# Moving the start addresses of the stationary operands from 224 to 192 bytes modulo 256 in a channel-attention and squared-ReLU kernel

## The chip, the core and the metric

The kernel runs on one core of one Trainium2 chip. The metric is the device time of one execution in microseconds (us). SBUF, the on-chip memory, is addressed per partition in bytes; "modulo 256" below speaks of those addresses. TensorE (PE) multiplies: each product has a **stationary** (fixed) operand, a block of 128 x 128 that is loaded into the array first, and a **moving** operand, whose columns then stream through. VectorE is DVE in the profile, ScalarE is ACT, GpSimd is POOL, and SP issues most DMAs.

## What is computed

Four batches of channel attention, and on its output a feed-forward layer with squared ReLU:

```python
B, N, C = 4, 6080, 256          # q, k, v: (B, N, C); w_in: (256, 2048); w_out: (2048, 256)
qn = q / (norm(q, axis=1) + 1e-06)
kn = k / (norm(k, axis=1) + 1e-06)
a = softmax(kn.transpose(0, 2, 1) @ qn / tau)      # 256 x 256 for each batch
x = (v @ a).reshape(B * N, C)
h = maximum(x @ w_in, 0.0)
out = (h * h) @ w_out
```

## The kernel before, in words

The softmax matrix is multiplied into `w_in` once for each batch, so that a token needs only `v @ W` (W is 256 x 2048), the ReLU, the square and the product with `w_out`. Every large product is made in three passes: an operand is split into a high part, rounded to float32r, and a low part, and hi x hi, lo x hi and hi x lo are summed in PSUM. Float32r products go through the array at one pass each; the few plain float32 products count twice in the trace.

The work has these stages. First come the Gram matrix of batch 0 (`gram`, plain float32, 256 columns), its norms (`ps_n`), the softmax, and W for batch 0 (`ps_w`, lines 749 to 766: the transposed exponentials `eT_hi` and `eT_lo` are stationary, a 512-column piece of `w_in` moves). Next come two blocks of 512 tokens in plain form (`ps_h` and `ps_o`, 512 columns). All further token blocks go through a two-by-two block scheme with seven products in place of eight, for W (`ps_b`, `ps_h`, `ps_c`) and for `w_out` (`ps_o`), with 256 moving columns, or 240 in the last two blocks of each batch. `PERIOD` (from line 1305) lists the steps of one group of this scheme by hand, and each engine keeps the order of the program. Beside it run the Gram matrices and the softmax of batches 1 to 3 (`gram<-qk_parts`, and `ps_w` with `dec_w` and `acc_w` moving).

Where a tile lies in SBUF follows from the pools, which are laid one behind another in the order in which they are opened: `smalls`, `const`, `wpool`, `wsums`, `pool`. A tile takes a multiple of 32 bytes in each partition, so that the one-column tiles `tau_sb` and `exp_bias` (lines 118 and 120) take 32 bytes each, as does `rinv_room` (line 125). With these in front, `wo_hi` begins at byte 17,888 = 69 x 256 + 224, and as the tiles behind it are multiples of 1,024 bytes, so do `wo_lo`, the weights `wf` (in `wpool`), `wS`, `wS_odd` and `wi` (in `wsums`) and the first tile of `pool`, `qk_parts`, at 224 modulo 256.

Lines 127 to 155 hold that first tile of `pool`: two halves of 4,096 bytes with a gap of `GAP = 8` words, 32 bytes, between them. For the Gram matrices the first half holds the k part (stationary, at 224) and the second the q part (moving). Because of the gap the second half, and every tile of `pool` behind it, begins at 0 modulo 256: the moving operands `v_hi`, `v_lo`, `A`, `s`, `dec_w` and `acc_w`, and also `eT_hi` and `eT_lo` (lines 733 and 734). A stationary block of 128 columns is 512 bytes and a moving one of 256 columns 1,024 bytes, so that slices of a tile keep its remainder. Only slices of 240-column tiles (960 bytes) begin at 0, 64, 128 or 192.

So the operands stand like this before (counts of products from the program, plain float32 ones left out):

| products | count | stationary at | moving at |
|---|---|---|---|
| 256 columns (`ps_b`, `ps_h`, `ps_c`, `ps_o`, `gram<-qk_parts`) | 13,578 | 224 | 0 |
| 240 columns (`ps_b`, `ps_h`, `ps_c`, `ps_o`, `ps_end`) | 2,694 | 224 | 0, 64, 128 or 192 |
| 512 columns (`ps_h`, `ps_o`) | 384 | 224 | 0 |
| 512 columns (`ps_w` of batch 0, `wi` moving) | 48 | 0 | 224 |
| 512 columns (`ps_w` of batches 1 to 3) | 144 | 0 | 0 |

The lines that decide this:

```python
tau_sb = const.tile([P, 1], F32, name="tau_sb")                      # 118
exp_bias = const.tile([P, 1], F32, name="exp_bias")                  # 120
GAP = 8                                                              # 128
return pool.tile([P, 2 * HALF + GAP], dt, tag="qk_parts", ...)       # 132
eT_hi = pool.tile([P, NC, C], F32R, tag="eT_hi", ...)                # 733
eT_lo = pool.tile([P, NC, C], F32R, tag="eT_lo", ...)                # 734
```

Of the kernel before, what the change touches and what calls it, by code (L numbers as in the profile page):

```python
# [10 lines left out]
F32 = mybir.dt.float32  # L11
F32R = mybir.dt.float32r
# [20 lines left out]
def kernel(  # L33
# [26 lines left out]
    P = 128  # L60
    B, N, C = q.shape
    F = w_in.shape[1]
    NC = C // P
# [35 lines left out]
    const = ctx.enter_context(tc.tile_pool(name="const", bufs=1))  # L99
    wpool = ctx.enter_context(tc.tile_pool(name="wpool", bufs=NG))  # L100
    wsums = ctx.enter_context(tc.tile_pool(name="wsums", bufs=1))
    pool = ctx.enter_context(tc.tile_pool(name="pool", bufs=2))
# [12 lines left out]
    make_identity(nc, ident)  # L115
    ones = const.tile([P, P], F32, name="ones")
    vector.memset(ones, 1.0)
    tau_sb = const.tile([P, 1], F32, name="tau_sb")

    exp_bias = const.tile([P, 1], F32, name="exp_bias")  # L120
    vector.memset(exp_bias, -896.0 * 2.0**23)

    for _ in range(7):
# [1 line left out]
    rinv_room = const.tile([P, NC], F32, name="rinv_room")  # L125

    HALF = NC * GRP
    GAP = 8

    def parts_room(name, dt):  # L130

        return pool.tile([P, 2 * HALF + GAP], dt, tag="qk_parts", name=name, bufs=1)

# [5 lines left out]
    def two_parts(name, dt, shape):  # L139

        room = parts_room(name, dt)
        halves = room[:, 0:HALF], room[:, HALF + GAP :]
        return [half.rearrange("p (a b) -> p a b", a=shape[1]) if len(shape) > 2 else half for half in halves]

    def rounded_qk(name):
# [3 lines left out]
        for at in (0, J * C):  # L149
            of_k = room[:, at : at + J * C]  # L150
            both = bass.AP(of_k.tensor, of_k.offset, [of_k.ap[0], [HALF + GAP, 2], of_k.ap[1]])
            parts.append(both.rearrange("p a (j c) -> p a j c", j=J))
# [438 lines left out]
    def attention(b):  # L591
# [41 lines left out]
        while behind:  # L633
            yield
        yield from softmax_and_W(b)
        while forming:
            yield
# [3 lines left out]
    def step(b, first, point):  # L641

        if b == 0:
            for i in range(first):
                yield i > 0
        else:
            yield
            yield from until(*ALSO.get(point, (point,)))

    def softmax_and_W(b):  # L650
# [79 lines left out]
                    ps_t[:, d * C + h * P : d * C + (h + 1) * P], e[:, h, d * P : (d + 1) * P], ident  # L730
                )
        yield from step(b, 2, "dve")
        eT_hi = pool.tile([P, NC, C], F32R, tag="eT_hi", name=f"eT_hi{b}", bufs=1)
        eT_lo = pool.tile([P, NC, C], F32R, tag="eT_lo", name=f"eT_lo{b}", bufs=1)
        ps_tv = ps_t.rearrange("p (d c) -> p d c", d=NC)
        vector.tensor_copy(eT_hi, ps_tv)
        vector.tensor_sub(eT_lo, ps_tv, eT_hi.bitcast(F32))
# [3 lines left out]
        for g in range(NG):  # L741
            if b == 0:
                while g not in wi_first:
                    yield
                hi, lo = wi_first.pop(g)
# [3 lines left out]
            else:  # L749
                hi, lo = wi_next.pop((b, g))  # L750
# [599 lines left out]
    weights = Weights()  # L1350
    rest = start_first()
    first = softmax_and_W(0)
    heads, squares_of_heads = head_products(), head_squares()
    stage = lambda item: lambda: weights.stage(item)
# [46 lines left out]
    for i in range(PAIR):  # L1401
        part = i % 2
        b, n, f = steps[i]
# [131 lines left out]
    b, n, _ = groups[END]  # L1535
# [53 lines left out]
```

## Time and profile before

| what | value |
|---|---|
| median of 3 runs | 2096.15 us (2094.93 to 2096.56) |
| span of the profiled execution | 2095.3 us |
| PE busy | 2090.3 us (100%) |
| PE weight loads (PEld) busy | 2054.0 us (98%) |
| DVE busy | 1904.2 us (91%) |
| ACT busy | 1878.4 us (90%) |
| POOL busy | 350.1 us (17%) |
| DMA | 549.78 MB, 262 GB/s on the mean |

The profiled execution's own time is its span, from the first to the last instruction; it lies 0.85 us under the median of the runs. The profile gives each matmul a duration of some 280 ns, but matmuls overlap in the array: what counts is the step from the start of one to the start of the next. The chain of waits shows it, since there a piece of n products of one kind stands with the time until the next kind takes over: time divided by n is the step. An L29 in a row is the line of a helper that records every operation, so that rows are told apart by the names of their tiles.

### The profile page before, as it was taken

The page shows a single profiled execution, that of the slowest core. Times are in us where ns is not written, and L with a number is a line of the kernel's source. Part 1 is how long each engine was busy: PE and PEld are TensorE (multiplying, and loading weights), DVE is VectorE, ACT ScalarE, POOL GpSimd, SP SyncE. Part 2 cuts the span into 40 slices and gives each one's busy share as a digit, 9 for nine tenths or more (in the row PEclk, how much of TensorE's full clock was granted, in tenths as well). Part 3 has the DMA queues.
Part 4 walks back from the last instruction along what each step waited for, and adds up shares of the span by engine and source line. Part 5 has one row for each costly group of instructions (what it writes and reads, how often), then busy time and mean ns, then how long its engine had stood idle before and what let it go on. Part 6 is the DMA issues. An engine that isn't in the chain of part 4 may idle for free.

```text
span 2095.3 us, 43463 instructions
## 1 busy us (share of the span) xinstructions
PE 2090.3 (100%) x17158; PEld 2054.0 (98%) x17158; DVE 1904.2 (91%) x2195; ACT 1878.4 (90%) x2379; POOL 350.1 (17%) x430
## 2 busy tenths in 40 slices
PE   9999999999999999999999999999999999999999
PEld 8789999999999999999999999999999999999999
DVE  7898999989999999989998999998999888888887
ACT  5888999889999999889989999998988988988987
POOL 0000121111122111111112111211121121121112
PEclk9999999999999999999999999999999999999999
DMA  9777887889999888789999988878999788787785
GB/s 359 225 227 272 256 258 250 239 260 308 304 279 306 268 256 256 237 247 293 290 298 275 317 251 265 251 241 250 289 280 301 236 240 255 233 246 246 234 241 155
DMA packets 258012, 549.78 MB, mean 262 GB/s; under 512 B 26672, under 2 KB 113072, under 8 KB 257808
## 3 DMA queue, kind: packets, MB, share of 16 engines
q1 hardware_dynamic: 201456, 469.02, 65.2%
q0 software_dynamic: 56352, 77.98, 18.8%
q8 instruction: 135, 2.21, 0.4%
q14 instruction: 69, 0.57, 0.1%
HBM read 433.59 MB, written 58.72 MB: 235 GB/s over the span
## 4 chain that ended last, share of the span: by engine, by line
PE 100%; DVE 0%; DVEq 0%; issue 0%
PE ps_o L29 45%; PE ps_c L29 18%; PE ps_h L29 14%; PE ps_b L29 12%; PE gram L29 7%; PE ps_w L29 2%; PE ps_end L29 0%; PE ps_first L29 0%; PE ps_n L29 0%; PE ps_t L29 0%; DVE x L29 0%; DVE end_o L29 0%; DVEq L1585 0%; DVE ones L29 0%; DVE exp_bias L29 0%
## 5 line engine op out<-in xcount | busy, mean ns | idle before, releaser
L29 DVE TENSOR_TENSOR x<-x 128x1024 f32<-128x1024 f32 (+2 forms) x549 | 465.3, 848 | 11.1
L29 PE MATMUL ps_c<-v_hi,wf 128*128 128x256 f32 (+1 forms) x2208 | 474.5, 279 | 0.2 <-DVE x L29 0.2
L29 POOL DMA_DIRECT2D o<-o x225 | 232.6, 1188 | 1391.2 <-ACT o L29 889.5
L29 DVE TENSOR_TENSOR s_lo<-x,s_hi 128x1024 fp32r<-128x1024 f32 (+1 forms) x366 | 441.9, 1208 | 15.9 <-ACT s_hi L29 15.4
L29 ACT ACTIVATE x<-x 128x1536 f32<-128x1536 f32 (+4 forms) x384 | 405.5, 1056 | 38.5 <-DVE x L29 35.3
L29 ACT CAST s_hi<-x 128x1024 fp32r<-128x1024 f32 (+1 forms) x366 | 383.0, 1046 | 53.9 <-DVE x L29 52.8
L29 DVE TENSOR_TENSOR A_lo<-x,A_hi 128x1536 fp32r<-128x1536 f32 (+2 forms) x183 | 313.6, 1714 | 82.0 <-ACT A_hi L29 67.4
L29 PEld LDWEIGHTS ps_c<-v_hi,wf 128*128 128x128 f32 x2208 | 375.5, 188 | 1.6 <-DVE x L29 0.9
L29 PE MATMUL ps_b<-v_hi,wf 128*128 128x256 f32 (+1 forms) x1472 | 315.9, 278 | 0.0
L29 PE MATMUL ps_h<-v_hi,wf 128*128 128x256 f32 (+1 forms) x1472 | 315.7, 278 | 0.0
L29 PE MATMUL ps_c<-v_lo,wf 128*128 128x256 f32 (+1 forms) x1104 | 307.3, 278 | 0.0
L29 ACT CAST A_hi<-x 128x1536 fp32r<-128x1536 f32 (+2 forms) x183 | 264.4, 1445 | 0.0
L29 PEld LDWEIGHTS ps_h<-v_hi,wf 128*128 128x128 f32 x1472 | 250.5, 188 | 0.0
L29 PEld LDWEIGHTS ps_b<-v_hi,wf 128*128 128x128 f32 x1472 | 250.3, 188 | 0.1
L29 PEld LDWEIGHTS ps_c<-v_lo,wf 128*128 128x128 f32 x1104 | 207.7, 188 | 0.1
L29 PE MATMUL ps_h<-v_lo,wf 128*128 128x256 f32 (+1 forms) x736 | 204.9, 278 | 0.0
L29 PE MATMUL ps_b<-v_lo,wf 128*128 128x256 f32 (+1 forms) x736 | 204.8, 278 | 0.0
L29 PE MATMUL ps_o<-A_hi,wo_hi 128*128 128x256 f32 (+1 forms) x897 | 192.8, 279 | 0.0
L29 PE MATMUL ps_o<-A_hi,wo_lo 128*128 128x256 f32 (+1 forms) x897 | 192.1, 278 | 0.0
L29 PE MATMUL ps_o<-A_lo,wo_hi 128*128 128x256 f32 (+1 forms) x897 | 191.8, 278 | 0.0
L29 PE MATMUL ps_o<-s_hi,wS_hi 128*128 128x256 f32 (+1 forms) x549 | 153.2, 279 | 0.0
L29 PE MATMUL ps_o<-s_hi,wS_lo 128*128 128x256 f32 (+1 forms) x549 | 153.2, 279 | 0.0
(172 smaller groups left out, 5153.5 us busy)
## 6 DMA issues: line engine op xcount, KB each, us to landing
wf<-wf_kept SPq DMA_DIRECT2D x368, 512.0 KB, 5.3
wf<-wf_kept SPq DMA_DIRECT2D x368, 384.0 KB, 4.9
o<-o POOLq DMA_DIRECT2D x114, 256.0 KB, 5.3
qk<-in_k SPq DMA_DIRECT2D x88, 256.0 KB, 5.3
qk<-in_q SPq DMA_DIRECT2D x88, 256.0 KB, 5.4
v<-in_vT SPq DMA_DIRECT2D x76, 256.0 KB, 4.8
out_T<-o POOLq DMA_DIRECT2D x152, 128.0 KB, 5.0
wf_kept<-wS SPq DMA_DIRECT2D x64, 256.0 KB, 7.2
```

Of the source, the lines that this page charges most:

```text
L29: return lambda *args, **kwargs: self.tc.keep_in_program_order(issue(*args, **kwargs))
```

## The change

It puts the two one-column tiles `tau_sb` and `exp_bias` into one tile of two columns, which takes 32 bytes in place of 64. All that lies behind moves down by 32 bytes: `wo`, `wf`, `wS`, `wS_odd`, `wi` and the k half of `qk_parts` now begin at 192 modulo 256. The gap in `qk_parts` grows from 32 to 64 bytes, so that the q half and the tiles behind it still begin at 0. The transposed exponentials `eT_hi` and `eT_lo` move from `pool` to `wsums`, and so from 0 to 192. In the table above 224 becomes 192, and the 0 of `eT` becomes 192 (with `wi` moving at 192 beside it in batch 0). The instructions of each engine, their order and their sizes stay the same.

```diff
-    tau_sb = const.tile([P, 1], F32, name="tau_sb")
-
-    exp_bias = const.tile([P, 1], F32, name="exp_bias")
+    single = const.tile([P, 2], F32, name="single")
+    tau_sb, exp_bias = single[:, 0:1], single[:, 1:2]
     vector.memset(exp_bias, -896.0 * 2.0**23)
...
     HALF = NC * GRP
-    GAP = 8
+    GAP = 16
...
-        eT_hi = pool.tile([P, NC, C], F32R, tag="eT_hi", name=f"eT_hi{b}", bufs=1)
-        eT_lo = pool.tile([P, NC, C], F32R, tag="eT_lo", name=f"eT_lo{b}", bufs=1)
+        eT_hi, eT_lo = (wsums.tile([P, NC, C], F32R, tag=f"eT_{i}", name=f"eT_{i}{b}", bufs=1) for i in ("hi", "lo"))
```

## Rows read from the trace of the kernel before

**Rows 1.** The page's part 1: busy time and share of the span.
```profile
span 2095.3 us, 43463 instructions
PE 2090.3 (100%) x17158; PEld 2054.0 (98%) x17158; DVE 1904.2 (91%) x2195; ACT 1878.4 (90%) x2379; POOL 350.1 (17%) x430
```

**Rows 2.** The page's part 4: the chain that ended last, by engine.
```profile
PE 100%; DVE 0%; DVEq 0%; issue 0%
```

**Rows 3.** The waits of PE: who waited for whom, us, times, longest.
```profile
PE ps_first L29 <- DVE exp_bias L29: 1.1, 1, 1.1
PE ps_c L29 <- DVE x L29: 0.2, 1, 0.2
```

**Rows 4.** Busy time by stretch, one row: busy us (count), clock, DMA share, GB/s.
```profile
1000.00:2080.00 1080.00, 1080.00 (x9256) 1076.55 (x9254) 978.31 (x1082) 980.27 (x1244) 202.95 (x247) 1.00 0.85 260
```

**Rows 5.** The chain, 917 to 933 us: start, us, what (256 columns; ps_w 512).
```profile
920.37 1.40 PE ps_o L29 x12
921.77 0.70 PE ps_c L29 x6
922.47 0.70 PE ps_h L29 x6
923.17 1.39 PE ps_w L29 x6
924.56 0.70 PE ps_o L29 x6
```

**Rows 6.** The chain, 1095 to 1102 us (240 columns; the last row 256).
```profile
1097.07 0.67 PE ps_c L29 x6
1097.74 0.67 PE ps_h L29 x6
...
1099.75 1.35 PE ps_o L29 x12
1101.10 0.70 PE ps_b L29 x6
```

**Rows 7.** The chain, 74 to 79 us (512 columns).
```profile
74.22 1.40 PE ps_h L29 x6
75.62 1.87 PE ps_w L29 x8
77.49 1.40 PE ps_o L29 x6
```

**Rows 8.** The chain's `ps_w` pieces in batches 1 to 3, four of 24.
```profile
513.50 1.40 PE ps_w L29 x6
934.36 1.38 PE ps_w L29 x6
1059.35 1.38 PE ps_w L29 x6
1490.85 1.39 PE ps_w L29 x6
```

**Rows 9.** The chain in the first stage: plain float32 products.
```profile
39.82 6.47 PE gram L29 x30
55.39 0.44 PE ps_t L29 x4
```

**Rows 10.** The waits of DVE for ACT, the three largest: us, times, longest.
```profile
DVE A_lo L29 <- ACT A_hi L29: 67.4, 105, 1.9
DVE qk_parts L29 <- ACT qk_parts L29: 16.4, 27, 0.9
DVE s_lo L29 <- ACT s_hi L29: 15.4, 36, 0.9
```

## The prediction

> **What bounds the kernel now.** The page's first part comes first [rows 1]: PE is busy for 2090.3 of 2095.3 us. Since matmuls overlap, that alone says little, so the chain that ended last comes next [rows 2]: all of it is PE, and DVE, queues and issue have 0%. The waits of PE agree [rows 3]: over the whole run it waited 1.1 us for its first operand and 0.2 us in the last group. [...] So the time is the number of products times their step, and a change that alters no instruction can alter the time only through the step, or through a new wait.
>
> The steps are read from the chain of waits. With 256 columns 12 products take 1.40 us [rows 5], 116.7 ns each, wherever one looks. With 240 columns 12 take 1.35 us and 6 take 0.67 [rows 6], 112.2 ns. With 512 columns 6 take 1.40 us [rows 7], 233.3 ns. Counting: 13,578 x 116.7 ns = 1584.0, 2,694 x 112.2 ns = 302.3 and 576 x 233.3 ns = 134.4, together 2020.7 us; the rest of the 2095.3 is plain float32 products, whose operands the change reaches only in part, the start and the end. This step is not what the columns alone would need. The float32 products of the first Gram matrix take 215.7 ns for 256 columns [rows 9]; if such a product is two passes of the same columns, one pass is 107.8 ns, and a float32r product loses 8.9 ns of its 116.7 to something. The question is whether that something depends on where the stationary operand begins.
>
> **The change part by part.** *Fewer constant tiles and the larger gap* by themselves cost nothing: the same memset, DMA and activations read and write other addresses, the constants are made before the first product, and the two columns of the new tile are written once each. If a reader of the bias column had now to wait for the load of tau, that would be one DMA in the first stage, of the order of the 1.1 us that PE waits there anyway [rows 3].
>
> *The stationary operands at 192 in place of 224.* The trace has no product with a stationary operand at 192, so its price has to come from neighbours. There are three.
>
> First, the products that multiply the softmax into w_in, in batches 1 to 3: six products of 512 columns, with the stationary operand at 0 and the moving one at 0. Their chain pieces take 1.39 us 14 times of 24, 1.38 six times and 1.40 twice [rows 5, 8]; one other holds a wait and one is cut by the window. The mean of the 20 at 1.38 and 1.39 is 1.387. The same shape with the stationary operand at 224 and the moving one at 0 takes 1.40 [rows 7]. So 0.013 us of 1.40 is gained, 0.93%, or 2.2 ns per product.
>
> Second, the same products in batch 0, stationary at 0 and moving at 224: 8 take 1.87 us [rows 7], 233.8 ns each (the two other such pieces have 1.86 and 1.87); nothing is gained to speak of. So it isn't the stationary operand's 0 alone that helps, nor the softmax step as such, but that both start on the same grid of 64 bytes: 224 is 32 past a multiple of 64, and where either operand stands at 224 the step is the slow one.
>
> Third, the products of 240 columns, whose moving operands begin at 0, 64, 128 and 192 with the stationary one always at 224: pieces of six with the moving operand at 128 and at 0 both take 0.67 us [rows 6]. A shift of one operand by multiples of 64 changes the step by less than the 0.01 us to which a piece is written, 1.7 ns per product. So it should matter little whether the distance between the two is 0, as in the first neighbour, or 192, as after the change; what should matter is that it is a multiple of 64.
>
> Together: after the change every float32r product is of the kind that was gained from in the first neighbour, those with 240 columns too. The size is open between two readings. If the gain goes with the columns, it is 0.93% of 2020.7 = 18.8 us. If it goes with the load of the stationary operand, which is the same 128 columns for each product, it is 2.2 ns x 16,848 products = 37.1 us. For the second speaks that a load fills nearly the whole of a 256-column product (PEld is busy 98% of the span [rows 1]) but only part of a 512-column one. No row separates them, so I take the middle, 28 us. The bounds of this price from the nearest rows are: from below, the two pieces at 1.40 [rows 8], a gain of nothing; from above, the whole 8.9 ns per 256 columns. A loss isn't excluded either, since distance 192 itself is in no row: the quarter-step rows leave up to 1.7 ns per product, 16,848 x 1.7 ns = 29 us.
>
> *The transposed exponentials from 0 to 192* take the 144 products of batches 1 to 3 out of the one kind that was fast. If distance 192 is worth nothing there, that loses 144 x 2.2 ns = 0.3 us; it is left in the range.
>
> *What is late next:* PE 28 us shorter leaves DVE's 1904.2 us at 92% of 2067 and ACT's 1878.4 at 91% [rows 1], so that they still fit. The sum is 2095.3 - 28 = 2067.3 in the profiled execution; the median lies 0.85 us above it, so 2068.
>
> **The rivals.** *(a) Nothing changes.* [...] The 0.01 us in the pieces of the softmax step could be their own. Against it: the piece with moving at 224 doesn't show the gain. Time 2096, within 4 us. [...]
>
> *(b) Slower: the quarter distance collides.* If memory is cut into four parts of 64 bytes in each 256, then at 224 a load always straddles two parts and gets past the moving stream half of the time, while at 192 it can fall into step with it and be held by a whole part at every turn. For: the distance of 192 is untried, and the pattern of starts within a step may be locked in step. Against: quarter shifts cost nothing visible at 240 columns. It decides where the stalls per product rise above the 8.9 ns that are lost now. Price: between the quarter-step bound of 1.7 ns, +29 us, and nothing; nearer the middle, as a piece of 12 halves that bound to 0.8 ns, so some +14 to +29 us: 2110 to 2125, with 2115 as its time.
>
> *(c) Much faster: the collisions vanish.* If all of the lost time comes from the two operands' meeting, 256 columns go to 107.8 ns, 512 to 215.7 by the same rate, and 240 to the 110 ns of the narrow transposes, four in 0.44 us [rows 9], below which a product with a load of 128 columns was not seen: 13,578 x 8.9 + 576 x 17.6 + 2,694 x 2.2 ns = 137 us, or 1959. DVE would then set the end: 1904.2 busy and its waits for ACT of 67.4, 16.4 and 15.4 us [rows 10] are 2003, so 2003 is what this gives. Against: the softmax pieces at distance 0 kept nine tenths of the loss. [...]
>
> **How the numbers follow.** A measurement of this kernel tells about 0.2%, 4.2 us, from no change. The forecast, a gain of 19 to 37 us, has 0.42; (c) 0.08; (a) 0.26; (b) and any other loss 0.24. So faster 0.50, within 0.2% 0.26, slower 0.24. The predicted time is that of the likeliest, 2068, whose own range is 2058 to 2080. The range for 8 in 10 has to take in no change, most of (b), and losses up to the quarter-step bound at its lower half, up to 2116; below it reaches halfway between the forecast and (c), 2035. That leaves out most of (c) and the dearer losses, some 0.18.
>
> **What would show it.** In the profile after, 12 products of 256 columns should take 1.37 to 1.39 us in place of 1.40, 6 of 512 columns 1.38 to 1.39, also in the plain stage at 74 us, and 12 of 240 columns 1.32 to 1.34. PE should still have all of the chain, with no more waits than before, at clock 1.00. The pieces of the softmax step in batches 1 to 3 should stay at 1.38 to 1.39. If the 256-column pieces stay at 1.40 while the softmax ones go back to 1.40, the distance has to be 0 and (a) holds; if they rise to 1.41 or more, (b); if DVE appears in the chain, (c). The forecast is wrong, too, if the step stays and the time moves, since then a wait or a transfer did it.

## The result, and the profile after

The changed kernel takes 2107.27 us on the median (2105.49 to 2107.45, 4 runs), the kernel before 2095.84 us (2094.93 to 2096.56, 4 runs): a ratio of 1.0053, 95% interval 1.0039 to 1.0068. It is slower by half a per cent, where a gain of 28 us was forecast. The profiled execution has a span of 2105.6 us, 10.3 more than before.

The page's first part, and the waits of PE after the change (who waited for whom, us, times, longest):

```profile
span 2105.6 us, 43463 instructions
PE 2100.4 (100%) x17158; PEld 2065.7 (98%) x17158; DVE 1905.2 (90%) x2195; ACT 1879.6 (89%) x2379; POOL 350.2 (17%) x430
```

```profile
PE ps_first L29 <- DVE single L29: 1.1, 1, 1.1
PE ps_c L29 <- DVE x L29: 0.2, 1, 0.2
PE ps_h L29 <- DVE w_lo L29: 0.2, 1, 0.2
```

Against [rows 1] only TensorE has grown, PE by 10.1 us and its weight loads by 11.7; DVE and ACT are within 1.2 us. PE waits no more than in [rows 3], but for 0.2 us once. So the time went into the step between products, and the chain shows into which. From four places of the changed kernel's chain (start, us, what): 512 columns, softmax step, 240 columns, 256 columns.

```profile
92.31 1.37 PE ps_o L29 x6
```

```profile
925.34 1.37 PE ps_w L29 x6
```

```profile
1098.03 0.68 PE ps_b L29 x6
```

```profile
1702.36 1.41 PE ps_o L29 x12
```

The plain products of 512 columns gained, even more than was forecast: 6 take 1.37 us against 1.40 in [rows 7]. In the softmax step the row shown stands for batch 2, whose pieces take 1.37 or 1.38; in batches 1 and 3 most stayed at 1.39 [rows 5, 8]. Products of 240 columns stayed [rows 6]. Those of 256 columns lost: 12 take 1.41 us against 1.40 [rows 5]. As a piece is written to 0.01 us, a count says it more sharply. The same 100 us in the middle of a long series, before and after (busy us and count of PE, PEld, DVE, ACT, POOL, clock, DMA share, GB/s):

```profile
1200.00:1300.00 100.00, 100.00 (x860) 100.00 (x859) 97.08 (x102) 95.30 (x118) 16.52 (x20) 1.00 0.81 256
```

```profile
1200.00:1300.00 100.00, 100.00 (x851) 100.00 (x850) 96.31 (x102) 93.64 (x114) 14.84 (x18) 1.00 0.80 257
```

Before 860 products run there, after 851, at the same clock of 1.00, 1% fewer. Taken from the starts of the products in the last long series (3,228 of them), the step was 116.7 ns before and is 117.8 after.

One row of the kernel before was overlooked for the forecast. Its first long series, 1,962 products between 164 and 397 us, had the slow step already, at the same addresses (the chain before, at 301 us):

```profile
301.75 1.41 PE ps_o L29 x12
```

The same stretch has 1.41 after the change as well. So the sum, taken from the step behind each product in the two traces, is: the 13,578 products of 256 columns take 10.95 us more, nearly all of it behind the first long series; the 384 plain products of 512 columns take 1.00 us less, and the 144 of the softmax step in batches 1 to 3 take 0.22 less. All else together is 0.57 more, which makes the 10.3 us between the two spans. The 1.00 is less than 384 x 4.6 ns, the gain of an undisturbed step from 233.4 to 228.8 ns, since the stretch has a few more long steps after the change.

Two theories stood first. **G**, which the prediction used: what counts is whether both operands start on the same grid of 64 bytes. **D**: the distance from the moving to the stationary operand, modulo 256, counts, each distance for itself. The distance is the start of the stationary operand minus that of the moving one. A third, **O**, was that other engines' traffic is needed for any difference. Later came a **theory of states**: a distance has one to three paces, and a series falls into one of them and keeps it.

### The profile page after: what moved, and what is told of

It is laid out like the page before. It is cut to its first block, busy times and chain, and to the rows that moved or that the text cites. A ratio compares the mean times of both kernels' runs of the same rounds, so it can differ in the third digit from the quotient of the medians.

```text
span 2105.6 us, 43463 instructions
## 1 busy us (share of the span) xinstructions
PE 2100.4 (100%) x17158; PEld 2065.7 (98%) x17158; DVE 1905.2 (90%) x2195; ACT 1879.6 (89%) x2379; POOL 350.2 (17%) x430
## 4 chain that ended last, share of the span: by engine, by line
PE 99%; ACT 0%; DVE 0%; issue 0%; DVEq 0%; ACTq 0%
PE ps_o L29 45%; PE ps_c L29 18%; PE ps_h L29 14%; PE ps_b L29 12%; PE gram L29 7%; PE ps_w L29 2%; PE ps_end L29 0%; PE ps_first L29 0%; PE ps_n L29 0%; ACT x L29 0%; PE ps_t L29 0%; DVE x L29 0%; DVE w_lo L29 0%; ACT A_hi L29 0%; ACT ps_c L29 0%
## 5 line engine op out<-in xcount | busy, mean ns | idle before, releaser
L29 ACT COPY x<-ps_c 128x512 f32<-128x512 f32 (+1 forms) x184 | 107.2, 582 | 53.1 <-PE ps_c L29 42.7
```

What stands on the lines that cost most here:

```text
L29: return lambda *args, **kwargs: self.tc.keep_in_program_order(issue(*args, **kwargs))
```

## The experiments

**TensorE alone: a table of start addresses.** A kernel of its own: operands at chosen offsets in two rooms, 48 products back to back for each pair of starts.

```diff
+def stretch(name, n, s, m):
+    ps = psum.tile([P, 512], F32, name=name, tag="ps")
+    for i in range(48):
+        a, b = 8 * s + 128 * (i % 4), 8 * m + 1024 * (i % 2)
+        nc.tensor.matmul(ps[:, 0:n], st[:, a : a + 128], mv[:, b : b + n], start=i == 0, stop=i == 47)
+    nc.vector.tensor_copy(zero[:, 0:n], ps[:, 0:n])
```

> This kernel computes nothing of the reference: it is TensorE alone, 48 float32r products back to back for each pair of start addresses (stationary at 0 to 224, moving at 0 to 224 modulo 256, in steps of 32) and several widths, with zeros written as its output. Theory G (a grid of 64 bytes): with 256 columns the step has two values, near 117.8 ns where stationary and moving start a multiple of 64 apart (as 192 and 0) and near 116.7 ns where they don't (as 224 and 0); with 512 columns the other way round, near 229 and 233. Theory D (the distance modulo 256): each of the eight distances has a value of its own, the same for pairs of equal distance, and 192 is among the slow ones. Theory O (other engines' traffic is needed): all 64 pairs take the same time within 0.3 ns, and the widths scale alike.

The chain of this kernel; in a name the first letter is the start of the stationary operand (a to h for 0 to 224 in steps of 32), the second that of the moving one.

```profile
21.55 5.76 PE ps_aa L55 x48
27.30 5.68 PE ps_ba L55 x48
32.98 5.66 PE ps_ca L55 x48
38.64 5.63 PE ps_da L55 x48
44.27 5.69 PE ps_ea L55 x48
49.96 5.75 PE ps_fa L55 x48
55.71 5.65 PE ps_ga L55 x48
61.36 5.66 PE ps_ha L55 x48
67.02 5.60 PE ps_ab L55 x48
...
186.34 5.47 PE ps_fd L55 x48
...
385.08 10.90 PE ps_aawide L55 x48
...
451.97 10.99 PE ps_gawide L55 x48
462.96 11.19 PE ps_hawide L55 x48
...
595.54 5.36 PE ps_gashort L55 x48
600.90 5.42 PE ps_hashort L55 x48
...
654.67 5.36 PE ps_hanabh L55 x48
```

Divided by 48, with nothing but a DVE copy between stretches beside it, at a mean granted clock of 0.965 over the whole run: 120.0 ns at distance 0, 118.3 at 32, 117.9 at 64, 117.3 at 96, 118.5 at 128, 119.8 at 160, 117.7 at 192. O falls: TensorE alone makes the differences. G falls: 0, 64, 128 and 192 differ by up to 2.3 ns. D, with one value for each distance, holds for most of the 64 pairs, but not for all: 224 has 117.9 in one stretch (h and a) and 116.7 in another (a and b, distance -32, the same 224), and 64 has 117.9 (c and a) and 114.0 (f and d). Taken from the starts of the products, six of the eight pairs at distance 64 run at 117.7 to 117.8 and two at 113.3.

Two more rows matter for the prediction. Products of 240 columns (*short*) take 111.7 ns at 192 and 112.9 at 224, and those of 128 columns 111.7 at 224 (the last row): at 240 columns the two distances are 1.2 ns apart, and 128 columns take hardly less. And with 512 columns (*wide*) 192 is faster than 224, 229.0 against 233.1 ns, the other way round than with 256 in the kernel. Distance 0 is the fastest of the eight there, 227.1 ns, and among the slowest with 256, 120.0.

**The whole kernel at other distances.** All take the changed kernel and alter a filler and the gap, moving operands at 0 unless said otherwise. For 0 (the others have a filler of 24, 32, 40, 48 or 56 words, for 32, 64, 96, 128 and 160, and the gap that brings the moving operands back):

```diff
     rinv_room = const.tile([P, NC], F32, name="rinv_room")
+    const.tile([P, 16], F32, name="filler")
...
-    GAP = 16
+    GAP = 0
```

> The changed kernel with a filler of 64 bytes in the constants and no gap: all fixed operands at 0, moving ones at 0. Theory G: as the changed kernel, 2107 us, 12 products of 256 columns in 1.41 us. Theory D: a value of its own, unlike 2096 and 2107. Theory O: as the changed kernel or as before, whatever other traffic decides.

> The changed kernel with a filler of 192 bytes and a gap of 128: all fixed operands at 128, moving ones at 0. Theory G: as the changed kernel, 2107 us. Theory D: a value of its own; distance 128 is half the period.

> The changed kernel with a filler of 160 bytes and a gap of 160: all fixed operands at 96, moving ones at 0. Theory G: as the kernel before, 2096 us, 12 products of 256 columns in 1.40 us. Theory D: a value of its own, unlike 2096.

> Fixed operands at 160, moving ones at 0. The table has 120.0 to 120.1 ns at this distance, as at distance 0, which took 2137 us in the kernel. Theory D: 2137 us, 12 products of 256 columns in 1.44 us. Theory S gives no such time to 160: between the 2108 of 96 and the 2120 of 128.

> Fixed operands at 32, moving ones at 0. The tables have one pace for this distance behind every lead-in, 118.33 ns, against a mean of 117.08 in the kernel before. Theory of states: 2096.5 + 13578 x 1.25 ns = 2113 us, 12 products of 256 columns in 1.42 us, the same in every series and every run. Theory G (grid of 64): 2096 us.

The paces are those of all four tables of TensorE alone, three of which come further down; each ratio is to the runs of the kernel before beside it.

| distance | pace in the tables, ns | kernel, us | ratio to before, 95% interval |
|---|---|---|---|
| 0 | 120.0 | 2136.88 | 1.0193 (1.0177 to 1.0208) |
| 32 | 118.3 | 2116.03 | 1.0098 (1.0083 to 1.0113) |
| 64 | 113.3 or 117.8 | 2079.00 | 0.9920 (0.9905 to 0.9935) |
| 96 | 117.3 or 118.7 | 2108.49 | 1.0058 (1.0041 to 1.0075) |
| 128 | 118.7 | 2120.53 | 1.0117 (1.0102 to 1.0132) |
| 160 | 120.0 | 2138.33 | 1.0198 (1.0183 to 1.0213) |
| 192 (the change) | 113.3 or 117.8 | 2107.27 | 1.0053 (1.0039 to 1.0068) |
| 224 (before) | 116.7 or 117.8 | 2095.84 | 1 |

One row each of the chains at 0, 32, 128 and 160, in the middle of the last long series:

```profile
1702.06 1.44 PE ps_o L29 x12
```

```profile
1702.15 1.42 PE ps_o L29 x12
```

```profile
1702.94 1.43 PE ps_o L29 x12
```

```profile
1704.04 1.44 PE ps_o L29 x12
```

Where a distance has one pace, the tables explain the kernels. At 32, for example, 11,616 products (the 13,578 less the 1,962 of the first long series) go from 116.7 to 118.3 and 1,962 from 117.8 to 118.3: 11,616 x 1.66 + 1,962 x 0.55 ns = 20.4 us on 2095.5 are 2115.9, and 2116.0 was measured. The 2113 that was expected had taken a mean of 117.08 for before, which contains its longer steps at the start of a series. At 160 the same sum gives 2096.6 + 43 = 2140 against 2138.3. G had put 0 and 128 with the change and 32, 96 and 160 with before; it is out.

**The distance or the address.** All fixed operands at 224 as before, the moving ones at 32 in place of 0, so that the distance is 192.

```diff
     rinv_room = const.tile([P, NC], F32, name="rinv_room")
+    const.tile([P, 8], F32, name="filler")
```

> All fixed operands stay at 224, as in the kernel before, but the moving ones begin at 32, so that the distance is 192, as in the changed kernel. Theory D (the distance alone counts): 2107 us, 12 products of 256 columns in 1.41 us. Theory S (the start of the stationary operand counts, 224 being good): 2096 us.

2105.63 us, ratio 1.0045 (1.0028 to 1.0062): the time of the change, not of before. The distance counts, not the address of the stationary operand (theory S); the kernel at 160 says the same, with the time of 0 and not one between those of 96 and 128. But its runs lie between 2100.0 and 2107.7, and the chain of the profiled one shows two paces in one execution:

```profile
441.57 1.36 PE ps_o L29 x12
...
1202.41 1.41 PE ps_o L29 x12
```

1.36 us are 113.3 ns a product, and 1.41 are 117.8 from the starts, for products of the same shape at the same distance. The table had raised the thought of states by its two paces at 64; here both occur within one execution of the kernel.

**Distance 64 in the kernel.** The filler has 32 words, the gap 48.

> Fixed operands at 64, moving ones at 0. The table of pairs had two paces at distance 64: 117.8 ns in six of eight stretches and 113.3 in two. Theory D with one pace for a distance: 2107 us. If the paces are states into which a stretch falls, and the kernel falls into the fast one: down to 2096 - 13578 x 3.3 ns = 2051 us; between the two if it changes from one to the other.

2079.00 us (2077.83 to 2084.21), ratio 0.9920 (0.9905 to 0.9935): this version beats both kernels; the one before had 2096.61 us beside it. It is between the two times that were expected, since both paces occur. Its chain, and the middle of the last series:

```profile
1200.51 1.36 PE ps_o L29 x12
...
1701.69 1.41 PE ps_o L29 x12
```

The same 100 us as above, 1200 to 1300, hold 885 products here, and 1700 to 1800 hold 852. From the starts of the products, a pace held for hundreds or thousands of products; where it changed, a wider or narrower product, or one longer step, stood between, and behind such a break came either pace. In the last series of 3,228 products the fast one held for some 350, past two such breaks, and was lost at the third.

**Are the paces states?** Two tables of TensorE alone. The first runs 192 products at a distance, in steps of 16, twice, and then takes turns between two starts; the second runs 60 products at distance 64 or 192 behind three lead-ins and behind none, one or two bridging products of 16 widths.

```diff
+for d, before, w, n in configs():
+    series(room("pre_" + name), (d, d, 160)[before], (240, 512, 256)[before], (24, 8, 24)[before])
+    if w:
+        series(room("bridge_" + name), d, w, n)
+    series(room("ps_" + name), d, 256, 60)
```

> TensorE alone again, nothing of the reference, zeros as output: 192 products of 256 columns in a row with the stationary operand at 0 to 240 in steps of 16, twice, moving at 0, then 96 products that take turns between two starts of the stationary operand, all 56 ordered pairs of multiples of 32. Theory D with one pace for a distance: both passes agree, steps of 16 lie between their neighbours, and a pair takes the mean of its two distances. If paces are states that a stretch falls into: passes differ by up to 4.4 ns at 64 and by 1 to 2 ns at 224, and pairs take values unlike the mean.

> TensorE alone, nothing of the reference, zeros as output: 60 products of 256 columns at distance 64 or 192, each time behind one of three lead-ins (24 products of 240 columns, 8 of 512, 24 of 256 at distance 160) and behind none, one or two bridging products of 16 to 512 columns. Theory of states: the 60 run at 113.3 or at 117.8 ns from end to end, which of the two depends on lead-in and bridge, and some width of bridge gives 113.3 behind every lead-in. Theory D with one pace for a distance: 113.3 throughout, since both passes of the second table gave that, with the 117.8 of the first table left unexplained.

In the first of them both passes agree, where the theory of states had expected them to differ; but each distance comes behind the same neighbour in both passes, all but the first, so this can't tell states from one pace for a distance. The chain of the first pass (e is 64, m is 192, o is 224):

```profile
112.81 21.77 PE ps_ee L52 x192
...
294.16 21.76 PE ps_mm L52 x192
...
338.32 22.40 PE ps_oo L52 x192
```

113.4, 113.3 and 116.7 ns: here even 192, the distance of the change, runs at the fast pace, where the first table had 117.7 for it. So the first table and this one disagree on the same distance, which one pace can't do. They ran on different chips, but the next table has both paces in one run. Steps of 16 don't all lie between their neighbours either: 80 has 118.8 ns between 113.3 at 64 and 117.3 at 96. The pairs that take turns have values unlike the mean of their two: 0 with 32 takes 116.7 ns, where the two alone have 120.0 and 118.3. In the second, the 60 products run at 113.3 or 117.8 ns and at nothing else: at distance 64, 62 of 99 stretches have the fast pace, at 192, 10 of 99. Lead-in and bridge pick one, but not by a rule that I could see: behind one bridge of 64 columns at distance 64 the lead-in of 240 columns leads into the fast pace (first row) and that of 512 into the slow one. Each of these rows holds one step of some 200 ns at its start, which is why a division by 60 gives 115.2 and 119.2 ns; the last 32 steps are at 113.3 and 117.8.

```profile
111.00 6.91 PE ps_bacb L50 x60
119.80 7.15 PE ps_bbcb L50 x60
```

At 64 no bridge at all, or two products of 16 columns, among others, gave the fast pace behind every lead-in; at 192 no bridge did. So of the two expectations for this run the theory of states holds, with its last clause for 64 alone, and one pace for a distance is out.

**A finer grid of distances.** 32 distances in steps of 8, each behind six lead-ins.

```diff
+LEADS = ((240, 9), (512, 4), (256, 11), (16, 5), (240, 14), (320, 7))
+for d, lead in [(8 * i, lead) for lead in range(6) for i in range(32)]:
+    series(room("pre_" + name), 160, *LEADS[lead])
+    series(room("ps_" + name), d, 256, 60)
```

> TensorE alone, nothing of the reference, zeros as output: 60 products of 256 columns at each of 32 distances in steps of 8 bytes, moving at 0, entered six times behind six different lead-ins. Theory of states: a distance has one to three paces of its own, the same whenever it comes, and the lead-in picks one; 64 and 192 have 113.3 and 117.8, 64 more often 113.3 and 192 more often 117.8; 224 has 116.7 and 117.8. If a distance between the multiples of 32 is at 113.3 behind all six lead-ins, it is worth trying in the kernel. Theory D with one pace for a distance: the six entries agree within 0.1 ns everywhere.

From the starts of the products, 18 of the 32 distances have one pace within 0.3 ns behind all six lead-ins, and 14 have two or three. At 192 all six are at 117.8, at 64 four at 113.3 and two at 117.8, at 224 three at 116.7 and three at 117.8. The slowest is 123.3, which 48 and 232 have behind two lead-ins each. One distance has the fast pace behind all six, 88 (the last letter, a to f, is the lead-in; the row of d holds one step of 204 ns, the others none over 124):

```profile
112.24 6.82 PE ps_bda L50 x60
...
370.43 6.84 PE ps_bdb L50 x60
...
631.49 6.83 PE ps_bdc L50 x60
...
891.57 6.96 PE ps_bdd L50 x60
...
1149.24 6.83 PE ps_bde L50 x60
...
1420.19 6.84 PE ps_bdf L50 x60
```

It wasn't tried in the kernel, whose tiles begin at multiples of 32 bytes, so that each fixed operand would need an offset inside its tile. Whether a kernel at 88 would beat the 2079 us of 64 is open.

**One part undone.** The changed kernel with the transposed exponentials back at 0.

```diff
-        eT_hi, eT_lo = (wsums.tile([P, NC, C], F32R, tag=f"eT_{i}", name=f"eT_{i}{b}", bufs=1) for i in ("hi", "lo"))
+        eT_hi = pool.tile([P, NC, C], F32R, tag="eT_hi", name=f"eT_hi{b}", bufs=1)
+        eT_lo = pool.tile([P, NC, C], F32R, tag="eT_lo", name=f"eT_lo{b}", bufs=1)
```

> The changed kernel with one part undone: the transposed exponentials go back to the pool, at 0; all other fixed operands stay at 192. They serve 192 products of 512 columns alone. Theory of states at 256 columns: the long series of 256 columns set the time, so nothing changes, 2107 us within 3. Theory E (the move of the exponentials costs the time): back to 2096 us.

2106.34 us, ratio 1.0052 (1.0036 to 1.0069): as the change. The exponentials' move costs nothing that can be measured; the loss sits in the other fixed operands.

## Why the prediction was wrong, by its own steps

**What bounds the kernel: right.** PE's steps made the whole time before and after; no wait appeared but 0.2 us once, and the constants' new tile cost nothing.

**The steps of the kernel before: wrong in one place, and it mattered.** The prediction has 116.7 ns "wherever one looks". The chain between 164 and 397 us has 1.41 us for 12 products, 117.8 ns, with the same addresses. Had that row been read, the step could not have been taken for a property of the addresses alone.

**The first neighbour: right for 512 columns.** The plain products of 512 columns gained 4.6 ns in an undisturbed step, where 2.2 was taken, and the first table has them fastest at distance 0 (227.1 ns, against 233.1 at 224).

**The second neighbour: the grid of 64 bytes is not what counts.** Distances 0, 64, 128 and 192 all put both operands on that grid, and the kernel takes 2137, 2079, 2121 and 2107 us with them.

**"Together": the step that failed.** "Every float32r product is of the kind that was gained from in the first neighbour" carried the gain from 512 columns over to 256, though the prediction has no row of 256 columns at any distance but 224. There the sign is the other one: distance 0 itself, where the gain had been read, costs products of 256 columns 3.3 ns (120.0 against 116.7; the kernel at 0 takes 2137 us). The change's distance 192 runs at 117.8 ns in the kernel's long series, before's 224 mostly at 116.7.

**The third neighbour failed too.** "A shift of one operand by multiples of 64 changes the step by less than" 1.7 ns was read from products of 240 columns and used for all. The table shows why these could not tell: at 240 columns the step is 111.7 ns at 192 and 112.9 at 224, within 1.2 ns of the 111.7 that 128 columns take at 224. At 256 columns a shift by multiples of 64 moves it from 120.0 (0) to 117.8 (192) and 118.7 (128), or down to 113.3 (64).

**The rivals.** (b), slower, was right in its sign and in taking the distance itself, untried, for the risk; that it locks with the moving stream no run shows. Its picture, four parts of 64 bytes, is not borne out: steps of 8 and 16 bytes count as well (118.8 ns at 80, 113.3 at 88, 117.3 at 96), and the kernel is fastest at 64. It also priced the loss at 14 to 29 us, where 11.4 came. (a) has no change, 2096 within 4 us: the step at 192 did change, from 116.7 to 117.8 ns in the last long series, and with other starts the kernel took from 2079 us (distance 64) to 2138 (160). (c) came nearest to showing what can be had: at 113.3 ns, which some series reach, 3.4 of the 8.9 ns that the prediction put down as lost are gone.

**The range** held the time, since it had room for most of (b), not by the mechanism that the point rests on; the point and the sign were wrong. What the theory of states adds is that the distance alone doesn't fix the sign. A forecast of 192 from the tables would have left open whether the series fall into 113.3 or 117.8 ns. With every series at the fast pace the change would have saved, by an estimate from these steps, 3.4 ns x 11,616 + 4.5 ns x 1,962 = 48 us.

What stays open is the cause beneath: whether and where the load of the stationary operand and the moving stream get in each other's way, and what picks the state at the start of a series. The tables show that no other engine's work is needed for it, but for a DVE copy between stretches; what inside TensorE or its way to SBUF makes the steps, no run shows.

## What to carry to other kernels

Where the chain is all PE, read its pieces over the whole span, and divide: here two steps for the same product at the same addresses, 117.8 and 116.7 ns, were the sign that a series keeps one of several paces. Measure a change of start addresses with TensorE alone first, at the width that the kernel uses and behind several lead-ins, since here 240 columns hid it (112.0 ns on the median before and after) and 512 had the other sign (229.0 ns at 192, 233.1 at 224). Such a table tells the paces; only the kernel itself tells which one its series take, where a distance has several. Here a distance of 64 bytes from the moving to the stationary operand modulo 256 gave 2079.00 us in place of 2096.61, without an instruction changed.

## What the runs showed of the hardware that was not expected

- The step of float32r products of 256 columns depends on the distance of the operands' starts modulo 256, by steps as fine as 8 bytes: from 113.3 ns at 88 to 120.0 at 0 and 160, and 123.3 in some entries at 48 and 232 (at 48 behind the first lead-in 60 products take 7.37 us), with a DVE copy between stretches and no other traffic but loads at the start and stores at the end.
- A distance can have two or three paces: 113.3 and 117.8 ns at 64 and at 192. A series can keep its pace over thousands of products: the last long one, of 3,228, has a mean step of 116.67 ns before and 117.78 after, and no step over 119. Behind the lead-ins and bridges 64 took the fast pace in 62 of 99 stretches, 192 in 10 of 99.
- From 128 to 240 columns the step is nearly flat at 192 and 224: 110.6 and 111.7 ns at 128, 111.7 and 112.9 at 240.
- At 512 columns distance 192 takes 229.0 ns and 224 takes 233.1, the reverse of their order in the kernel at 256, 117.8 and 116.7 in the last long series.
